# Padding keys of the later head pairs by one bf16 product over three exact parts

## The chip, the core and the metric

The kernel runs on one core of a Trainium2 chip. The metric is the device time of one execution in microseconds, taken as the median of several runs. Five engines work side by side, each through its own instruction list in order: TensorE (PE in the profile, with its weight loads as PEld), VectorE (DVE), ScalarE (ACT), GpSimd (POOL) and SyncE (SP, which here only issues DMAs). They meet through semaphores.

## The reference, cut to what matters

Two parts follow each other. The first is attention in chunks of 32 tokens, for 4 x 8 = 32 heads of 768 tokens and 64 channels. Each chunk sees eight learned memory keys of its head and the keys from 16 tokens before it to 8 tokens behind it:

```python
for c in range(nc):
    l_start = max(0, c_start - left_ctx)
    r_end = min(S, c_end + right_ctx)
    k_full = np.concatenate([mem_k, k[:, :, l_start:r_end]], axis=2)
    v_full = np.concatenate([mem_v, v[:, :, l_start:r_end]], axis=2)
    scores = scale * np.matmul(q_c, k_full.transpose(0, 1, 3, 2))
    a = softmax(scores)
    out[:, :, c_start:c_end] = np.matmul(a, v_full)
```

The second is a mixture of eight experts with one expert for each of the 3072 tokens: a gate (a product with `w_gate` plus a bias by modality) chooses the expert, and the token goes through that expert's two layers, 512 to 1024 to 512 channels, scaled by the gate. All is in fp32.

## The kernel before, in words

**Stages.** Attention goes over 16 pairs of heads (`u`, 0 to 15), each in two halves (`hf`) of twelve chunks, so that the loop counter `i` runs over 32 units and two more. Pair n's keys are turned at `i` = 2n - 2. While the pairs run, the gate of each batch of four pairs is computed in between (`route`). At the end of the attention stage the experts begin: a static list of slots of 256 tokens, with weights loaded by number of the expert, and rows gathered and scattered by GpSimd.

**Order.** Every engine's order is written out by hand: the order of the calls in the Python source is the order on each engine. A DMA on SP waits until the DMA eight places before it is done, since eight semaphores go round.

**The loop of a pair.** In the first half of pair u (even `i`) TensorE does: `scores` (L328), the transposes of the softmax input (`trans_p`, L345), the keys of the next pair (`trans_k`, L310 and L314), the transposes of the normalized output (`trans_x`, L382), the product with the values (`attend`, L357). In the second half (odd `i`) the place of the keys is taken by the queries of the next pair (`trans_q`, L292). PSUM has four banks `tr` that go round, so `trans_k` of head 1, `trans_k` of head 0 and the two halves of `trans_q` take the same banks in turn: the second half of `trans_q` can't start before ScalarE has copied head 0's keys out.

**The step that is changed.** `trans_k` puts 384 turned keys of a head into a bank by three transposes (L310), and into the gaps at both ends of the row ("pads", 16 columns, four different ones repeated) a product of `mkp`, all memory keys as 128 rows of 128, with four columns of the identity (`ident`) as the selector (L314). The result is four memory keys' channels, exact in fp32, there where the first and the last chunk would else read outside the sequence. `store_k` (L320) then copies windows of the bank into the block-diagonal key tile `kbd`, for pairs 5 and later all four copies on ScalarE. For a fp32 product the trace has two weight loads and two matmuls.

**GpSimd in the attention stage** does, for each pair: `share_v` (L271, two copies, one for a head, each behind the DMA that brings the values), the store of the output (`store_x`, L375), `mem_keys` (L302, two copies of memory keys into `kbd`). At `i` = 8 it also does `bias_rows` (L239 to L243).

**SP in the attention stage** issues, for each pair: six loads of values (L255 to L257), two copies of the memory values (L264), one load of keys and one of queries (L94). At `i` = 1 four small loads stand among them (L171 to L174).

Of the kernel before, what the change touches and what calls it, by code (L numbers as in the profile page):

```python
# [9 lines left out]
F32 = mybir.dt.float32  # L10
F32R = mybir.dt.float32r
U16 = mybir.dt.uint16
BF16 = mybir.dt.bfloat16
# [8 lines left out]
P = 128  # L22
# [23 lines left out]
def tile_chunk_attention_top1_moe(  # L46
# [14 lines left out]
    nc = tc.nc  # L61
# [13 lines left out]
    ld = c_ld.enter_context(tc.tile_pool(name="ld", bufs=3))  # L75
# [8 lines left out]
    def bank():  # L84
        return ps.tile([P, 512], F32, name="tr", tag="tr", bufs=4)
# [3 lines left out]
    def load_qk(u):  # L89
        r0 = u * 2 * S  # L90
        q2s[u] = ld.tile([P, 6, 2 * D], F32, name="q2")
        k2s[u] = ld.tile([P, 6, 2 * D], F32, name="k2")
        for t, f in ((k2s[u], kf), (q2s[u], qf)):
            nc.sync.dma_start(t.rearrange("p (h i) e -> p h (i e)", h=2), f[r0:r0 + 2 * S].rearrange("(h p j) d -> p h (j d)", h=2, p=P))  # L94
# [12 lines left out]
    mkp = pers.tile([P, P], F32, name="mkp")  # L107
# [11 lines left out]
    for h in range(2):  # L119
        r = slice(64 * h, 64 * h + 64)  # L120
        nc.scalar.copy(kbds[1][r, :, 1 - h], zero[r].unsqueeze(2).to_broadcast([64, NCH, 64]))

    ident = const.tile([P, P], F32, name="ident")
# [50 lines left out]
        nc.sync.dma_start(rows_b[N // P:], bass.AP(tensor=m_bias.tensor, offset=0, ap=[[0, 1], [0, N // P], [1, E]]))  # L174

    memT = pers.tile([P, 16, NMEM], F32, name="memT")
    iota5 = const.tile([P, 5, 27], F32, name="iota5")
    iota3 = const.tile([P, 3, 65], F32, name="iota3")
    rev = const.tile([P, 1, E], F32, name="rev")
# [68 lines left out]
    def load_v(u):  # L248
        vw = vws[u % NVW]
        for h in range(2):  # L250
            hh = 2 * u + h
            r0 = 64 * h

            src = bass.AP(tensor=vf.tensor, offset=(hh * S + 8) * D, ap=[[D, 32], [32 * D, NCH - 1], [1, D]])
            nc.sync.dma_start(vw[r0 + 24:r0 + 56, h, 0:NCH - 1, 0:D], src)  # L255
            nc.sync.dma_start(vw[r0 + 24:r0 + 48, h, NCH - 1, 0:D], vf[hh * S + S - 24:hh * S + S])
            nc.sync.dma_start(vw[r0 + 16:r0 + 24, h, 0, 0:D], vf[hh * S:hh * S + 8])  # L257

    def load_mv(u):
        vw = vws[u % NVW]  # L260
        for h in range(2):
            hh = 2 * u + h
            r0 = 64 * h
            nc.sync.dma_start(vw[r0 + 56:r0 + 64, h].rearrange("p c d -> p (c d)"), mvx[hh // 16][8 * (hh % 16):8 * (hh % 16) + 8].rearrange("p c d -> p (c d)"))  # L264
# [39 lines left out]
    def trans_k(u):  # L304
        k2 = k2s.pop(u)
        for h in (1, 0):
            hh = 2 * u + h
            t = kts[u, h] = bank()
            for i in range(3):
                nc.tensor.transpose(t[:, 9 + i:9 + i + 3 * P:3], k2[:, 3 * h + i, :], ident)  # L310

            pads = bass.AP(tensor=t.tensor, offset=t.offset + 1, ap=[list(t.ap[0]), [392, 2], [1, 8]])
            mem_sel = ident[:, 4 * hh:4 * hh + 4].unsqueeze(1).unsqueeze(1)
            nc.tensor.matmul(pads, mkp, mem_sel.to_broadcast([P, 2, 2, 4]), start=True, stop=True)  # L314

    def store_k(u, h, j, copy):
        tt = kts[u, h][64 * j:64 * j + 64]
# [55 lines left out]
    def store_x(u):  # L373
        b, g = divmod(u, 4)
        nc.gpsimd.dma_start(xd[b * S:(b + 1) * S, g * P:(g + 1) * P].rearrange("(t p) c -> p t c", p=P), xbs[u])  # L375
# [378 lines left out]
    def conv(i, eng=None):  # L754
        nc.scalar.copy(wh[i], raw[i])  # L755
        (eng or nc.vector).tensor_sub(wl[i], raw[i], wh[i].bitcast(F32))  # L756
# [6 lines left out]
    def fetch(rows, part):  # L763
        for t in range(2):
            nc.gpsimd.indirect_dma_start(  # L765
                out=xg[t][:, part], out_offset=None, in_=rows, in_offset=bass.IndirectOffsetOnAxis(ap=gx[:, t:t + 1], axis=0))

    def gather(row, gates=True, between=()):
        if row < 2:
            src, reg, rows = table, regsb[0:1, 2:3] if row else regs0[0:1, 1:2], N - S  # L770
        else:
            src, reg, rows = tab_i, (regs1 if row < NSURE else regs)[row:row + 1, 2:3], N
        col = nc.values_load(reg, engines=[mybir.EngineType.Pool], min_val=0, max_val=E * HI,
                             skip_runtime_bounds_check_because="clamped to the table on chip")
        nc.gpsimd.tensor_copy(ix, src[:, ds(col, 2)])
        nc.gpsimd.tensor_scalar(gx, ix, float(rows - 1), None, op0=ALU.min)
        fetch(xd[0:rows], slice(0, DM))
        for step in between:
            step()
        if flipped(row):  # L780
            for t in range(2):
                flip(planes[t], xg[t], xpl[:, :, t * P:(t + 1) * P])
        if gates:
            fetch(gd[0:rows], slice(DM, XW))
# [146 lines left out]
    load_qk(1)  # L931
    load_v(1)
    trans_k(0)
    t = ps.tile([P, 512], F32, name="av", tag="av", bufs=2)
    for h in range(2):
# [34 lines left out]
    for i in range(n + 2):  # L970
        live = i < n
        u, hf = units[i] if live else (NU, i % 2)
# [101 lines left out]
        if live and hf == 0 and u >= 1:  # L1074
            if u - 1 + NVW < NU:
                load_v(u - 1 + NVW)
                load_mv(u - 1 + NVW)
            if u + 4 < NU:
                load_qk(u + 4)
        if (u, hf) == (NU - 2, 1):  # L1080
            c_ld.close()
            xp = ctx.enter_context(tc.tile_pool(name="xp", bufs=1, side="right"))
            ix = xp.tile([P, 2], I32, name="ix")
            gx = xp.tile([P, 2], I32, name="gx")
            xg = [xp.tile([P, XW], F32, name=f"xg{t}") for t in range(2)]
            xt = xp.tile([P, 4, 2, 256], F32R, name="xt")
            xth, xtl = xt[:, :, 0], xt[:, :, 1]
            w1h, w1l = [xp.tile([P, 8, 512], F32R, name=f"w1{i}") for i in range(2)]
            hh, hl = [xp.tile([P, 8, 256], F32R, name=f"h{i}") for i in range(2)]
            for f in range(8):  # L1090
                raw[f] = xp.tile([P, 512], F32, name=f"raw{f}")
                wh[f], wl[f] = w1h[:, f], w1l[:, f]
            flat = vws[1].rearrange("p h c d -> p (h c d)"), kbds[0].rearrange("p c h m -> p (c h m)")
            old = [t[:, k * 512:(k + 1) * 512] for t in flat for k in range(6)]
            raw[8:16] = old[0:8]
            load_w(0, 0, 0)
            with nc.allow_non_contiguous_dma(reason="one gate per token"):
                nc.sync.dma_start(*chosen.pop())
            gather(0, gates=False)
            for f in range(4, 8):  # L1100
                nc.gpsimd.memset(raw[f][0:1, 0:1], 0.0)
            load_w(0, 0, 1)
        elif (u, hf) == (NU - 1, 1):
            conv(0)
            other = second()
            fetch(gd[0:N - S], slice(DM, XW))
            for f in range(8, 16):
                nc.gpsimd.memset(raw[f][0:1, 0:1], 0.0)
            load_w(0, 1)
            store_x(NU - 3)  # L1110
            store_x(NU - 2)
# [220 lines left out]
```

## Time and profile before

| what | value |
|---|---|
| time, median of 3 runs | 430.8 us (430.32 to 432.37) |
| the profiled execution, its own time | 429.93 us |
| its span in the trace | 428.1 us |
| TensorE busy | 412.1 us (96%) |
| VectorE, ScalarE, GpSimd busy | 335.0, 300.2, 234.2 us |
| granted TensorE clock | 0.996 of full speed on the mean |

The span is the stretch from the first to the last instruction; 1.8 us of the execution lie around it. The attention stage is about the first 123 us, the experts are the rest. A busy share tells little about what a change is worth: what counts is which engine the others wait for at each place, which the chain of waits and the timelines of the engines tell.

### The profile page before, as it was taken

What the parts mean: (1) busy time and instruction counts of PE and PEld (TensorE: products, weight loads), DVE (VectorE), ACT (ScalarE), POOL (GpSimd) and SP (SyncE); (2) the same over time, 40 slices, a digit from 0 to 9 for tenths busy, and PEclk for the clock granted to TensorE, in tenths of its full rate; (3) what the DMA queues carried; (4) which work ended last, traced back from release to release, by engine and by line L of the source; (5) the groups of instructions that cost most, each with busy time, mean ns of one, the idle gap of its engine ahead of it and who ended that gap; (6) DMA issues with size and microseconds to landing.
All of it is one profiled execution on the core that took longest, in us unless ns stands there. A gap on an engine that the chain in (4) does not pass through costs nothing.

```text
span 428.1 us, 11395 instructions
## 1 busy us (share of the span) xinstructions
PE 412.1 (96%) x3867; PEld 342.2 (80%) x3870; DVE 335.0 (78%) x800; ACT 300.2 (70%) x597; POOL 234.2 (55%) x320
## 2 busy tenths in 40 slices
PE   7998999999999999999999999999999999999993
PEld 4776788877867888899898888888888778888882
DVE  6899588588787789858979887868985887978750
ACT  7787778687655557557566867868784778878750
POOL 8967678669584409666753466452706566520101
PEclk9999999999999999999999999999999999999998
DMA  9889999999659500335423667979938323320101
GB/s 218 184 217 246 229 273 201 258 255 212 133 132 312 176 2 2 100 99 76 92 82 52 270 192 167 332 207 334 277 143 253 98 72 84 86 64 2 50 3 55
DMA packets 82543, 66.81 MB, mean 156 GB/s; under 512 B 50659, under 2 KB 71339, under 8 KB 82476
## 3 DMA queue, kind: packets, MB, share of 16 engines
q1 hardware_dynamic: 75276, 46.36, 44.4%
q0 software_dynamic: 6784, 19.50, 14.5%
q8 instruction: 33, 0.54, 0.6%
q14 instruction: 34, 0.28, 0.2%
q10 hardware_dynamic: 416, 0.13, 0.1%
HBM read 84.64 MB, written 12.76 MB: 228 GB/s over the span
## 4 chain that ended last, share of the span: by engine, by line
PE 57%; issue 16%; DVE 10%; DMA 6%; ACT 5%; POOL 4%; POOLq 0%; SPq 0%; ACTq 0%; DVEq 0%
PE av L856 11%; PE tr L844 9%; PE sc L856 8%; PE tr L825 7%; PE av L357 4%; PE tr L828 4%; PE sc L328 3%; ACT kbd L320 3%; PE tr L382 2%; PE tr L345 2%; DMA xpm<-xw 2%; PE tr L292 2%; PE tr L310 1%; DMA out_dram<-o,ix_now 1%; POOL xg L765 1%
## 5 line engine op out<-in xcount | busy, mean ns | idle before, releaser
L756 DVE TENSOR_TENSOR w<-raw,w 128x512 fp32r<-128x512 f32 x96 | 67.4, 746 | 4.1 <-ACT w L755 3.6
L825 PE MATMUL tr<-xt,w 128*128 128x512 f32 x256 | 70.3, 396 | 0.0
L856 PE MATMUL av<-wh,h 128*128 128x512 f32 x192 | 62.5, 398 | 0.0
L271 POOL COPY vw<-vw 24x1472 f32<-24x1472 f32 x32 | 45.0, 1408 | 18.9 <-DMA vw<-in_v_dram 17.5
L755 ACT CAST w<-raw 128x512 fp32r<-128x512 f32 x96 | 53.9, 619 | 0.6 <-DMA raw<-in_moe_w_dram 0.6
L856 PE MATMUL sc<-wh,h 128*128 128x512 f32 x160 | 51.7, 398 | 0.0
L825 PEld LDWEIGHTS tr<-xt,w 128*128 128x128 f32 x256 | 44.3, 189 | 7.5 <-DVE hs L834 0.7
L844 PE MATMUL tr<-xt,w 128*128 128x256 f32 x384 | 48.2, 285 | 1.2 <-DVE xt L820 0.7
L844 PEld LDWEIGHTS tr<-xt,w 128*128 128x128 f32 x384 | 46.8, 191 | 2.7 <-DVE xt L820 0.9
L320 ACT COPY kbd<-tr 64x672 f32<-64x672 f32 x57 | 44.6, 782 | 2.9 <-PE tr L314 1.3
L828 PEld LDWEIGHTS tr<-xt,w 128*128 128x128 f32 x256 | 39.3, 189 | 5.4
L856 PEld LDWEIGHTS av<-wh,h 128*128 128x128 f32 x192 | 36.1, 188 | 8.4 <-issue 0.2
L861 POOL DMA_INDIRECT out_dram<-o,ix_now x22 | 24.5, 1112 | 29.8 <-ACT o L860 24.1
L828 PE MATMUL tr<-xt,w 128*128 128x256 f32 x256 | 40.7, 281 | 0.0
L856 PE MATMUL av<-wl,h 128*128 128x512 f32 x96 | 38.1, 397 | 0.2 <-DVE wl L756 0.2
L834 DVE TENSOR_TENSOR hs<-tr,hs 128x256 f32<-128x256 f32 x64 | 26.8, 419 | 14.4 <-ACT hs L831 14.3
L856 PEld LDWEIGHTS sc<-wh,h 128*128 128x128 f32 x160 | 30.1, 188 | 7.1 <-issue 0.2
L835 ACT ACTIVATE h<-hs 128x256 fp32r<-128x256 f32 x64 | 26.8, 419 | 12.7 <-DVE hs L834 11.6
L837 DVE TENSOR_TENSOR wl<-vw,wh 128x512 fp32r<-128x512 f32 x48 | 34.0, 709 | 2.1
L838 DVE SCALAR_TENSOR_TENSOR h<-hs,h 128x256 fp32r<-128x256 f32 x64 | 27.3, 426 | 7.7 <-ACT h L835 7.7
L765 POOL DMA_INDIRECT xg<-xd,gx x24 | 27.6, 1149 | 10.3 <-issue 5.5
L347 ACT ACTIVATE PT<-tr 128x384 f32<-128x384 f32 x32 | 15.8, 495 | 23.2 <-PE tr L345 23.0
(265 smaller groups left out, 911.1 us busy)
## 6 DMA issues: line engine op xcount, KB each, us to landing
raw<-in_moe_w_dram SPq DMA_DIRECT2D x96, 256.0 KB
vw<-in_moe_w_dram SPq DMA_DIRECT2D x72, 256.0 KB
k<-in_k_dram SPq DMA_DIRECT2D x16, 384.0 KB
q<-in_q_dram SPq DMA_DIRECT2D x16, 384.0 KB
xd<-xb POOLq DMA_DIRECT2D x16, 384.0 KB, 5.9
kbd<-in_moe_w_dram SPq DMA_DIRECT2D x24, 256.0 KB
vw<-in_v_dram SPq DMA_DIRECT2D x32, 184.0 KB
xall<-in_moe_w_dram SPq DMA_DIRECT2D x4, 1024.0 KB
```

Source lines behind the costliest of these rows:

```text
L271: nc.gpsimd.tensor_copy(vw[r0:r0 + 24, h, 1:NCH, 0:D], vw[r0 + 32:r0 + 56, h, 0:NCH - 1, 0:D])
L320: copy(dst.rearrange("p c (i j) -> p c i j", j=2)[:, :, :, j], win)
L755: nc.scalar.copy(wh[i], raw[i])
L756: (eng or nc.vector).tensor_sub(wl[i], raw[i], wh[i].bitcast(F32))
L765: nc.gpsimd.indirect_dma_start(out=xg[t][:, part], out_offset=None, in_=rows, in_offset=bass.IndirectOffsetOnAxis(ap=gx[:, t:t + 1], axis=0))
L825: nc.tensor.matmul(ph, wh[f][:, c * P:(c + 1) * P], xt[:, c].rearrange("p a n -> p (a n)"), start=(c == 0), stop=False, skip_group_check=True)
L828: nc.tensor.matmul(ph[:, 0:256], wl[f][:, c * P:(c + 1) * P], xth[:, c], start=False, stop=(c == 3), skip_group_check=True)
L834: nc.vector.tensor_add(hs, ph[:, 0:256], hs)
L837: nc.vector.tensor_sub(wl[w], raw[w], wh[w].bitcast(F32))
L838: nc.vector.scalar_tensor_tensor(hl[:, f], hs, 0.0, hh[:, f].bitcast(F32), op0=ALU.max, op1=ALU.subtract)
L844: nc.tensor.matmul(ph, w[f][:, c * P:(c + 1) * P], x[:, c, :], start=(n == 0), stop=(n == 11))
L856: nc.tensor.matmul(pos[t], x, w[8 + f], start=(f == 0 and n == 0), stop=(f == 7 and n == 2))
```

## The change

From pair 6 on, the sixteen pad columns come from a bf16 product. Each fp32 memory key is split into three bf16 parts whose sum is the key (first the key rounded to bf16, then the rest rounded, then what is left). The parts stand in `bits`: partitions 0 to 31, 32 to 63 and 64 to 95 hold part one, two and three of eight heads' keys (32 rows of 128), with four such groups side by side for 32 heads, and zeros in the last 32 partitions. `pick3` is a 32 x 32 identity three times over, so that one product adds the three parts of the four rows that it picks. Pairs 0 to 5 keep the fp32 product.

The parts are made at the beginning: three DMAs of 64 KB on SP at `i` = 1, behind the load of keys and queries of pair 4, bring the same 32 rows to three places of `mem3`; GpSimd splits them in three steps at the ends of `i` = 4, 6 and 8.

```diff
     memT = pers.tile([P, 16, NMEM], F32, name="memT")
+    mem3 = ld.tile([96, 4, P], F32, name="mem3", bufs=1)
+    bits = ld.tile([P, 4, P], BF16, name="bits", bufs=1)
+    pick3 = ld.tile([P, 32], BF16, name="pick3", bufs=1)
+
+    def load_mem3(k):
+        src = bass.AP(tensor=mem_k.tensor, offset=0, ap=[[P, 32], [32 * P, 4], [1, P]])
+        nc.sync.dma_start(mem3[32 * k:32 * k + 32], src)
+
+    def split_mem3(step):
+        pool, two, three = nc.gpsimd, slice(32, 64), slice(64, 96)
+        if step == 0:
+            pool.memset(bits, 0.0)
+            pool.memset(pick3, 0.0)
+            for k in range(3):
+                pool.tensor_copy(pick3[32 * k:32 * k + 32], ident[32 * k:32 * k + 32, 32 * k:32 * k + 32])
+            pool.tensor_copy(bits[0:96], mem3)
+        elif step == 1:
+            pool.tensor_sub(mem3, mem3, bits[0:96])
+            for r in (two, three):
+                pool.tensor_copy(bits[r], mem3[r])
+        else:
+            pool.tensor_sub(mem3[three], mem3[three], bits[three])
+            pool.tensor_copy(bits[three], mem3[three])
...
             pads = bass.AP(tensor=t.tensor, offset=t.offset + 1, ap=[list(t.ap[0]), [392, 2], [1, 8]])
-            mem_sel = ident[:, 4 * hh:4 * hh + 4].unsqueeze(1).unsqueeze(1)
-            nc.tensor.matmul(pads, mkp, mem_sel.to_broadcast([P, 2, 2, 4]), start=True, stop=True)
+            if u < 6:
+                mem_sel = ident[:, 4 * hh:4 * hh + 4].unsqueeze(1).unsqueeze(1)
+                nc.tensor.matmul(pads, mkp, mem_sel.to_broadcast([P, 2, 2, 4]), start=True, stop=True)
+            else:
+                mem_sel = pick3[:, 4 * (hh % 8):4 * (hh % 8) + 4].unsqueeze(1).unsqueeze(1)
+                nc.tensor.matmul(pads, bits[:, hh // 8], mem_sel.to_broadcast([P, 2, 2, 4]), start=True, stop=True)
...
+        if i == 1:
+            for k in range(3):
+                load_mem3(k)
+        if i in (4, 6, 8):
+            split_mem3(i // 2 - 2)
```

Three places show how the order moves. First TensorE, before the change, at the keys of pair 6 (`i` = 10); `k_603` is the key tile of that pair, and the brackets name the engines or DMA queues that the instruction waits for:

```order
L345 MATMUL tr<-ident,sb 128x128 x2
L310 MATMUL tr<-ident,k_603 128x128 [waits DMAHW2_49,PE_49]
L310 MATMUL tr<-ident,k_603 128x128 x2
L314 MATMUL tr<-ident,mkp 128x2x8
L310 MATMUL tr<-ident,k_603 128x128 [waits PE_49]
L310 MATMUL tr<-ident,k_603 128x128 x2
L314 MATMUL tr<-ident,mkp 128x2x8
L382 MATMUL tr<-ident,xb 128x128 [waits DVE_49,Activation_49]
```

The same place after it, with the lines' new numbers (L310 is L333 now, L314 is L341, L345 is L372, L382 is L409):

```order
L372 MATMUL tr<-ident,sb 128x128 x2
L333 MATMUL tr<-ident,k_609 128x128 [waits DMAHW5_49,PE_49]
L333 MATMUL tr<-ident,k_609 128x128 x2
L341 LDWEIGHTS bits [waits Pool_49]
L341 MATMUL tr<-pick_148,bits 128x2x8
L333 MATMUL tr<-ident,k_609 128x128 [waits PE_49]
L333 MATMUL tr<-ident,k_609 128x128 x2
L341 LDWEIGHTS bits
L341 MATMUL tr<-pick_148,bits 128x2x8
L409 MATMUL tr<-ident,xb 128x128 [waits DVE_49,Activation_49]
```

The fp32 product became one weight load and one matmul, and the first weight load waits for GpSimd; no other wait of TensorE is added in the whole program.

GpSimd before, from the memory keys of pair 3 (L302, `kbd_111`) to the values of pair 5 (L271, `vw_114`):

```order
L302 COPY kbd_111<-memT 64x24x8 x2
L271 COPY vw_112<-vw_112 24x23x64 x2
L375 DMA xd<-xb 128x6x128
L302 COPY kbd_110<-memT 64x24x8 x2
L271 COPY vw_113<-vw_113 24x23x64 x2
L375 DMA xd<-xb 128x6x128
L302 COPY kbd_111<-memT 64x24x8 x2
L239 MEMSET mods 25x128
L240 CAST mods<-mod_i 24x128
L241 TENSOR_TENSOR bias_b<-bias_b 24x8
L243 TENSOR_TENSOR rows_b<-bias_b,ident 24x192
L271 COPY vw_114<-vw_114 24x23x64 x2
```

GpSimd after, first from the memory keys of pair 3 (now L325) to the second step of the split:

```order
L325 COPY kbd_111<-memT 64x24x8 x2
L188 MEMSET bits 128x512
L189 MEMSET pick_148 128x32
L191 CAST pick_148<-ident 32x32 x3
L192 CAST bits<-mem_146 96x512
L294 COPY vw_112<-vw_112 24x23x64 x2
L402 DMA xd<-xb 128x6x128
L325 COPY kbd_110<-memT 64x24x8 x2
L194 TENSOR_TENSOR mem_146<-mem_146,bits 96x512
```

The first step of the split stands ahead of the values of pair 3 (now L294), and its last copy, from the loaded keys, holds the engine until the three DMAs are there. Then, still after the change, the second and the third step:

```order
L194 TENSOR_TENSOR mem_146<-mem_146,bits 96x512
L196 CAST bits<-mem_146 32x512 x2
L294 COPY vw_113<-vw_113 24x23x64 x2
L402 DMA xd<-xb 128x6x128
L325 COPY kbd_111<-memT 64x24x8 x2
L262 MEMSET mods 25x128
L263 CAST mods<-mod_i 24x128
L264 TENSOR_TENSOR bias_b<-bias_b 24x8
L266 TENSOR_TENSOR rows_b<-bias_b,ident 24x192
L198 TENSOR_TENSOR mem_146<-mem_146,bits 32x512
L199 CAST bits<-mem_146 32x512
L294 COPY vw_114<-vw_114 24x23x64 x2
```

The second step stands ahead of the values of pair 4, the third behind `bias_rows` and ahead of the values of pair 5; the copy at L199 is the one that TensorE waits for. On SP the three DMAs stand between the queries of pair 4 and the values of pair 3, and nothing else moves; VectorE and ScalarE keep their lists.

## Rows read from the trace of the kernel before

**Rows 1.** Page: shares of the chain that ended last, by engine.
```profile
PE 57%; issue 16%; DVE 10%; DMA 6%; ACT 5%; POOL 4%; POOLq 0%; SPq 0%; ACTq 0%; DVEq 0%
```

**Rows 2.** Chain that ended last (start us, length us, work): unit 7, pair 10, rank products.
```profile
36.46 0.80 PE av L357 x24
...
75.71 0.33 PE tr L310 x3
76.04 0.13 PE tr L314 x2
76.17 0.37 PE tr L310 x3
76.54 0.13 PE tr L314 x2
...
80.27 0.74 PE tr L292 x6
...
89.73 0.13 PE tr L577 x6
```

**Rows 3.** TensorE's timeline at the next pair's queries (start, length, instructions, idle before).
```profile
49.78 0.92 PE L292 MATMUL tr<-ident,qr 128*128 128x128 f32 x6
...
65.40 0.55 PE L292 MATMUL tr<-ident,qr 128*128 128x128 f32 x3 [0.25 <-ACT kbd L320]
...
72.40 1.05 PE L292 MATMUL tr<-ident,qr 128*128 128x128 f32 x6
```

**Rows 4.** ScalarE's timeline in pairs 6 and 8.
```profile
46.00 3.22 ACT L320 COPY kbd<-tr 64x672 f32<-64x672 f32 x4
...
61.65 0.49 ACT L347 ACTIVATE PT<-tr 128x384 f32<-128x384 f32 x1 [1.32 <-PE tr L345]
62.16 3.19 ACT L320 COPY kbd<-tr 64x672 f32<-64x672 f32 x4
```

**Rows 5.** TensorE's timeline: first pad product of pair 6.
```profile
45.55 0.29 PE L314 MATMUL tr<-ident,mkp 128*128 128x16 f32 x2
```

**Rows 6.** GpSimd's timeline, 32 to 43 us.
```profile
32.06 1.41 POOL L271 COPY vw<-vw 24x1472 f32<-24x1472 f32 x1 [0.24 <-DMA vw<-in_v_dram]
...
34.34 0.74 POOL L302 COPY kbd<-memT 64x192 f32<-64x192 f32 x2
37.51 2.88 POOL L271 COPY vw<-vw 24x1472 f32<-24x1472 f32 x2 [2.43 <-DMA vw<-in_v_dram]
...
42.84 0.51 POOL L243 TENSOR_TENSOR rows_b<-bias_b,ident 24x192 f32<-24x192 f32 x1
```

**Rows 7.** GpSimd's groups by line and form (count, busy us, mean ns of one, idle before).
```profile
L271 POOL COPY vw<-vw 24x1472 f32<-24x1472 f32 x32 | 45.0, 1408 | 18.9 <-DMA vw<-in_v_dram 17.5
...
L673 POOL TENSOR_SCALAR a<-iota,ac,tokm 128x192 fp32r<-128x192 f32 x10 | 10.7, 1070 | 0.0
L302 POOL COPY kbd<-memT 64x192 f32<-64x192 f32 x28 | 10.1, 361 | 5.9 <-PE sc L328 4.5
...
L243 POOL TENSOR_TENSOR rows_b<-bias_b,ident 24x192 f32<-24x192 f32 x1 | 0.5, 505 | 0.1
...
L241 POOL TENSOR_TENSOR bias_b<-bias_b 24x8 f32<-24x8 f32 x1 | 0.2, 196 | 0.0
```

**Rows 8.** DMA view, 20 to 50 us, all packets; and SP's timeline, one issue.
```profile
DMA packets 9751, 7.07 MB, mean 236 GB/s; under 512 B 6826, under 2 KB 9392, under 8 KB 9744
...
25.08 0.42 SPq L255 DMA_DIRECT2D vw<-in_v_dram  x1
```

**Rows 9.** VectorE's timeline: a small copy beside GpSimd's copy, and a maximum.
```profile
30.71 1.13 DVE L223 CAST tab_i<-table 128x2 int32<-128x2 f32 x1
...
36.31 0.55 DVE L336 TENSOR_REDUCE mx<-sc 128x6 f32<-128x384 f32 x1
```

**Rows 10.** GpSimd's timeline ahead of that, and TensorE's at unit 7.
```profile
30.41 1.41 POOL L271 COPY vw<-vw 24x1472 f32<-24x1472 f32 x1 [3.15 <-DMA vw<-in_v_dram]
...
37.85 0.55 PE L345 MATMUL tr<-ident,sb 128*128 128x128 f32 x3
```

## The prediction

> **What bounds the kernel now.** I read the page first: the chain that ended last is TensorE's for 57% and ScalarE's for 5% [rows 1]. That says that time taken from TensorE can count, not that it does. So I went to the chain in order of time, in the attention stage, where the changed products stand, and then to the timelines of the engines beside TensorE, to see at each pair who arrives last.
>
> Around the pad products the chain is TensorE's in pair 10: three transposes, 0.13 us for the two records of a fp32 pad product, three transposes, 0.13 us again [rows 2]. But the next thing that TensorE does with the same PSUM banks is to turn the queries of that pair, and the second half of that waits until ScalarE has copied the keys out. In pair 8 TensorE stands idle there for 0.25 us, behind ScalarE's copies [rows 3]; pairs 7, 11, 12 and 14 read the same, with 0.21, 0.24, 0.22 and 0.55 us. ScalarE in turn is one unbroken run: from the exponential at 61.65 us through four copies until 65.35 [rows 4]. That run starts with trans_p, ahead of the keys, so it doesn't feel how long a pad product takes. In these pairs ScalarE sets the pace, and TensorE has time to spare. In pair 9 the six query transposes take 1.05 us in place of some 0.92 [rows 3], the same wait hidden in a longer group; pairs 13 and 15 read alike. Only in pairs 6 and 10, alike, do the six run through without a wait [rows 3]: there TensorE has the gate's products to do in between, ScalarE is done at 49.22 us [rows 4], and the second three transposes start at about 50.15 (half of the 0.92 us group behind 49.78), so ScalarE is early by about 0.9 us.
>
> **What it removes.** Twenty fp32 pad products, two in each of ten pairs. In pair 10 the stretch is 0.33 + 0.13 + 0.37 + 0.13 = 0.96 us; six transposes alone take 0.74 [rows 2]. Two pad products are worth 0.22 us, 0.11 each. What takes their place is like the rank products, bf16 with a weight load of their own, of which six take 0.13 us, 0.022 each [rows 2]. The trace has no bf16 product among fp32 transposes: I bound it by 0.022 below and by the fp32 price 0.11 above (then nothing is gained), and take 0.025 as the rank products are nearest in form. The saving is 2 x (0.11 - 0.025) = 0.17 us for a pair, bounds 0 and 0.18. Over ten pairs that is 1.7 us of TensorE's time. On the path lie pairs 6 and 10 alone: **0.34 us**. In the other eight the same 0.17 us only makes the wait for ScalarE longer.
>
> **What it adds on SP and the DMA engines.** Three issues and 3 x 64 KB = 197 KB, ahead of the values of pair 3. At the stretch's 236 GB/s [rows 8] these are 0.83 us. Bounds: 0 if they fill a gap, 1.3 us if SP's three issues, 0.42 us each [rows 8], are what counts. I take 0.83. Who waits: GpSimd, whose second copy for pair 3 was let go by its DMA at 32.06 [rows 6], so now at 32.9. TensorE needs the values at 36.46, when pair 3's product begins [rows 2], and GpSimd is done with them 1.41 us after its DMA, at 34.3: the delay is covered by some two microseconds.
>
> **What it adds on GpSimd.** A copy costs (1408 - 361) / (1472 - 192) = 0.82 ns per element over some 0.2 us, so 0.62 us for 512 elements; a two-input operation (505 - 196) / (192 - 8) = 1.68 ns per element, so 1.04 us for 512 [rows 7]. Step one (two fills, three small copies, one copy of 512) lies in the 3.15 us in which GpSimd waits for the values of pair 3 [rows 10], and costs nothing there but the arrival of its own three DMAs, which the 0.83 us hold already. Step two is 1.04 + 2 x 0.62 = 2.3 us, step three 1.04 + 0.62 = 1.66 us.
>
> **The new wait.** TensorE's weight load for pair 6 waits for step three. I follow GpSimd: values of pair 3 done at 32.9 + 1.41 = 34.3; store and memory keys, 1.6 us (from 32.06 + 1.41 = 33.47 to 34.34 + 0.74 = 35.08 before) [rows 6], until 35.9; step two until 38.3. The values of pair 4 were there at 37.51 [rows 6], now at 38.3, so this costs nothing more. From 37.51 to 43.35 (42.84 + 0.51) GpSimd ran without a stop [rows 6]; now that stretch is 38.35 to 44.2. Step three with its gaps is 1.8 us: bits are there at 46.0. TensorE wants them at 45.55 [rows 5]. It waits **0.45 us**, in pair 6, where TensorE sets the pace, and behind the weight load stand head 0's keys, trans_x, the product with the values and the gate's products. Bounds: nothing if the DMAs delay nothing (GpSimd 0.8 us earlier); on the other side a subtraction could cost as much per element as the dearest row, 1070 ns for 192 [rows 7], so 2.85 us in place of 1.04, and bits would be there at 46.0 + 2 x 1.81 = 49.6, a wait of 4.1 us. I take the two-input row, the same operation in fp32.
>
> **The sum.** 0.45 - 0.34 = +0.1 us. Against the profiled execution (429.93 us) that is 430.0; the median of the runs is 0.9 us above it, so on the median 430.8 + 0.1 = 430.9.
>
> **The shared port.** VectorE's copy of two columns took 1.13 us, from 30.71 to 31.84, and GpSimd's copy ran from 30.41 to 31.82 [rows 9, 10]. So VectorE can stand behind a GpSimd instruction, and GpSimd has more of them now. The Trainium skill, "SBUF — State Buffer", section "Who interferes with whom", says that a VectorE instruction in a two-port mode and a GpSimd instruction shut each other out for a whole instruction. It speaks against this change; by that rule the time would be the third rival's. The trace agrees for the copy of two columns.
>
> **Rivals.** *All pairs pay.* If the waits for ScalarE shrink with TensorE's work, or bits come in time and every pair gives 0.17 us, the gain is 1.7 us: 429.1, at the bound of 0.18 a little under. For it speaks that the chain names the pad products in most pairs; against it, the waits in eight of ten pairs.
> *Bits in time, VectorE freed.* Step one's own wait moves the values of pair 3 to about 31.2 us. The copy of two columns, which lost 1.0 us behind them [rows 9], is then through before. VectorE is on the chain there; with 0.34 us from TensorE and 0.7 of the 1.0 kept this is 429.8. It needs bits before 45 us, 1 us earlier than my sum.
> *VectorE blocked.* Step two's subtraction begins at 35.9, just when three small VectorE operations stand ahead of the maximum of unit 7 at 36.31 [rows 9]. If they wait until it ends, the maximum is 0.9 us late and the transposes at 37.85 [rows 10] by 0.5; four small operations near 28 us meet step one's copies, some 0.6 together. Pair 6 is then 1.1 us late by VectorE, which hides the wait for bits: 1.1 - 0.34 = +0.8, 431.6.
> *Bits very late, slower.* The single mechanism is GpSimd's price for mixed fp32 and bf16 operands. At the upper bound the wait is 4.1 us: +3.7, 434.5; half way it is 2.3 us: +1.9, 432.7. It decides for slower at all from bits at 45.9 us on, and for a loss of 0.5% from 48.0. Against it: copies and two-input operations are the cheaper rows.
> *The product isn't cheaper.* Then nothing is saved and 0.45 us is lost: 431.3.
>
> **How the numbers follow.** Forecast (429.9 to 431.6, nearly no change) 0.47; all pairs pay 0.12; bits in time with VectorE freed 0.11; VectorE blocked 0.12; bits very late 0.13; product not cheaper 0.05. The likeliest gives 430.9. The range from 429.0 to 432.8 takes in all but the far half of "all pairs pay" and of "bits very late", and the 2 us by which the runs of before differ among themselves. 0.5%, about what a measurement of this kernel can tell from no change, is 2.15 us, so under 428.6 and over 433.0. Faster by more needs all pairs and something else on top, the freed VectorE: 0.08. Slower by more is half or more of "bits very late" with a part of the blocked case: 0.12. The rest, 0.80, is within.
>
> **What would show it.** In the new trace: the pad product as one record of a bf16 product, with some 0.03 us on the chain, shows the price; the idle time of TensorE ahead of the query transposes at 0.35 to 0.45 us in pairs 7, 8, 11 and 12 shows that the saving went into the wait for ScalarE; a wait of TensorE for GpSimd of about half a microsecond at 45 to 46 us, once, shows the third step late; two subtractions at 1.0 us and copies at 0.6 show GpSimd's prices. I am wrong if those waits for ScalarE stay as they are and the stage ends earlier by over a microsecond; or if the subtractions take two microseconds and more; or if the values of pair 3 or 4 now hold TensorE, which no term of mine allows.

## The result: 0.5% slower, and where the time stands in the new profile

The changed kernel takes 433.53 us on the median of 22 runs (429.96 to 435.53), the kernel before 431.42 us on the median of 22 runs. The ratio is 1.0052, interval 1.0032 to 1.0073: some 2.2 us slower. The prediction was 430.9 in a range from 429.0 to 432.8; the measured time lies beyond its slow end. Two further measurements, on two chips, gave 1.0048 (1.0028 to 1.0067) and 1.0017 (0.9987 to 1.0046); the second can't be told from no change.

The profiled execution took 430.76 us, only 0.8 us above that of before. So there are two questions: where the 0.8 us come from, and why the medians lie 2.1 us apart.

In the new page, the shares of the chain that answer to [rows 1]:

```profile
PE 51%; issue 15%; DVE 10%; ACT 8%; DMA 6%; POOL 6%; SPq 1%; POOLq 0%; ACTq 0%; DVEq 0%
```

TensorE's share fell from 57% to 51%, ScalarE's rose from 5% to 8%, GpSimd's from 4% to 6%. The lines have moved: L310 is now L333, L314 is L338 (fp32) and L341 (bf16), L292 is L315, L320 is L347. TensorE's timeline after the change, as [rows 5] and [rows 3] (start, length, instructions, idle before); the first keys of pair 7 and of pair 15 stand at 55.81 and 117.57 us:

```profile
45.27 0.49 PE L333 MATMUL tr<-ident,k 128*128 128x128 f32 x3
47.40 0.18 PE L341 MATMUL tr<-pick,bits 128*128 128x16 bf16 x1 [1.64 <-POOL bits L199]
...
55.81 0.49 PE L333 MATMUL tr<-ident,k 128*128 128x128 f32 x3
...
59.79 0.55 PE L315 MATMUL tr<-ident,qr 128*128 128x128 f32 x3 [0.44 <-ACT kbd L347]
...
117.57 0.49 PE L333 MATMUL tr<-ident,k 128*128 128x128 f32 x3
```

The same keys of pairs 7 and 15 before the change:

```profile
54.21 0.49 PE L310 MATMUL tr<-ident,k 128*128 128x128 f32 x3
...
115.99 0.49 PE L310 MATMUL tr<-ident,k 128*128 128x128 f32 x3
```

The first bf16 product of pair 6 waits 1.64 us for the last step of the split. Then, in pairs 7 and 8, the wait for ScalarE's copies is 0.44 us (59.79 and 66.97) where it was 0.21 and 0.25 [rows 3]. From pair 7's first key transpose to pair 15's it takes 61.76 us, and 61.78 before (54.21 to 115.99): the cheaper product brought nothing there. At pair 7 the changed kernel is 1.60 us late (55.81 against 54.21), at pair 15 1.58 us. Of this 0.8 us is left at the end; what gives back the rest, behind the attention stage, was not tried.

GpSimd's timeline, as [rows 6]:

```profile
33.05 1.81 POOL L294 COPY vw<-vw 24x1472 f32<-24x1472 f32 x1 [1.13 <-DMA vw<-in_v_dram]
...
36.57 1.16 POOL L194 TENSOR_TENSOR mem<-mem,bits 96x512 f32<-96x512 f32 x1
37.80 1.25 POOL L196 CAST bits<-mem 32x512 bf16<-32x512 f32 x2
39.11 3.09 POOL L294 COPY vw<-vw 24x1472 f32<-24x1472 f32 x2
...
45.20 1.15 POOL L198 TENSOR_TENSOR mem<-mem,bits 32x512 f32<-32x512 f32 x1
46.42 0.93 POOL L199 CAST bits<-mem 32x512 bf16<-32x512 f32 x1
```

The parts are ready at 47.35 us; the prediction had 46.0.

### The profile page after: what moved, and what is told of

Read it like the earlier page. It is cut to its first block, busy times and chain, and to the rows that moved or that the text cites. A ratio compares the mean times of both kernels' runs of the same rounds, so it can differ in the third digit from the quotient of the medians.

```text
span 428.8 us, 11371 instructions
## 1 busy us (share of the span) xinstructions
PE 409.3 (95%) x3850; PEld 339.4 (79%) x3850; DVE 330.0 (77%) x800; ACT 300.1 (70%) x597; POOL 245.2 (57%) x331
## 3 DMA queue, kind: packets, MB, share of 16 engines
q0 software_dynamic: 6784, 19.50, 14.2%
## 4 chain that ended last, share of the span: by engine, by line
PE 51%; issue 15%; DVE 10%; ACT 8%; DMA 6%; POOL 6%; SPq 1%; POOLq 0%; ACTq 0%; DVEq 0%
PE av L883 11%; PE tr L871 8%; PE sc L883 8%; PE tr L852 7%; ACT kbd L347 5%; PE tr L855 4%; PE av L384 2%; PE sc L355 2%; POOL xg L792 2%; DMA xpm<-xw 2%; DMA vw<-in_moe_w_dram 2%; PE tr L372 1%; PE tr L315 1%; DMA out_dram<-o,ix_now 1%; PE tr L409 1%
## 5 line engine op out<-in xcount | busy, mean ns | idle before, releaser
L783 DVE TENSOR_TENSOR w<-raw,w 128x512 fp32r<-128x512 f32 x96 | 65.6, 728 | 4.1 <-ACT w L782 3.6
L294 POOL COPY vw<-vw 24x1472 f32<-24x1472 f32 x32 | 46.1, 1440 | 11.9 <-DMA vw<-in_v_dram 10.5
L347 ACT COPY kbd<-tr 64x672 f32<-64x672 f32 x57 | 44.6, 782 | 4.1 <-PE tr L341 1.6
L817 POOL COPY planes<-xg 128x1024 uint16<-128x1024 uint16 x18 | 22.4, 1255 | 18.5 <-DMA xg<-xd,gx 18.5
```

Of the source, the lines that this page charges most:

```text
L294: nc.gpsimd.tensor_copy(vw[r0:r0 + 24, h, 1:NCH, 0:D], vw[r0 + 32:r0 + 56, h, 0:NCH - 1, 0:D])
L347: copy(dst.rearrange("p c (i j) -> p c i j", j=2)[:, :, :, j], win)
```

## Experiments: the wait, the clock behind it, the split, and ScalarE

Three theories stood against each other. Theory A: the time is the wait in pair 6 and what follows from it. Theory B: the loads and GpSimd's work cost by themselves. Theory C: the difference of the medians is scatter of the clock.

**The changed kernel again (e1).** No edit.

> The changed kernel once more, as the measure for the others of this set. Theory A (the wait for bits): its trace shows TensorE idle for 1.5 to 1.8 us once, ahead of the first bf16 pad product, and its median is 1.0 to 2.5 us above the kernel before. Theory B (GpSimd's and the DMA engines' added work slows the stage by itself): the same sum, but only part of the 1.6 us stands at that wait. Theory C (the difference between the medians, 2.1 us, against 0.8 between the two profiled executions, is scatter of the granted TensorE clock): the ratio comes out under 1.003 this time.

Measured: 433.21 us against 431.18, ratio 1.0048. Its profiled execution, span 432.2 us, shows what the first one didn't. TensorE's timeline, and a table by stretches (length, busy time of PE, PEld, DVE, ACT, POOL with counts, then the granted clock, DMA share, GB/s):

```profile
46.25 0.49 PE L333 MATMUL tr<-ident,k 128*128 128x128 f32 x3
48.53 0.18 PE L341 MATMUL tr<-pick,bits 128*128 128x16 bf16 x1 [1.79 <-POOL bits L199]
...
49.46 1.53 PE L384 MATMUL av<-vw,PT 128*32 128x130 f32 x24
50.77 2.43 PE L561 MATMUL tr<-xall,wg 128*32 128x384 f32 x16
53.02 0.83 PE L355 MATMUL sc<-kbd,qT 128*32 128x128 f32 x24
```
```profile
49.30:52.70 3.40, 3.40 (x41) 1.81 (x42) 0.92 (x3) 3.31 (x6) 3.23 (x5) 0.50 1.30 267
52.70:60.00 7.30, 7.30 (x136) 6.31 (x132) 3.84 (x13) 3.70 (x9) 4.61 (x6) 1.00 1.07 241
```

Behind 1.79 us of idle TensorE, up to 48.53 us, the granted clock is still 1.00 until 49.30, then 0.50, which is 1.2 GHz, for 3.4 us. The product with the values there takes 1.31 us from start to start and the gate's products 2.25, in place of 0.69 and 1.29 at 1.00 in the first trace: 1.6 us lost on top of the wait. Where the clock falls, only a trace shows; of the other executions the mean clock alone is on record, and 3.4 us at half the clock take some 0.004 from it (an estimate: 1.7 of 432 us). The kernel before has 0.995 to 0.999 in all 35 runs of this set; the changed kernel has 0.994 or less in 15 of its first 22 runs and in 9 of these 12. These 24 have a median of 433.8 us, the ten others 431.8. So the clock does scatter, as C says, but in this set it is low in most runs of the changed kernel and in none of the kernel before.

This trace also shows something that speaks for theory B. Pair 6's keys begin at 46.25 us, 1.0 us later than before, still ahead of the new wait. GpSimd began the second copy of pair 3's values at 34.69 us, where the first trace had 33.05, and TensorE stood idle for its memory keys, 0.70 us ahead of 37.76 and 0.28 us ahead of 45.07. GpSimd's and TensorE's timelines:

```profile
34.69 1.42 POOL L294 COPY vw<-vw 24x1472 f32<-24x1472 f32 x1 [0.46 <-DMA vw<-in_v_dram]
...
37.76 0.86 PE L355 MATMUL sc<-kbd,qT 128*32 128x128 f32 x24 [0.70 <-POOL kbd L325]
```

**From pair 7 on (e2), the split without its use (e3), bias_rows earlier (e4).**

```diff
-            if u < 6:
+            if u < 7:       (e2)
+            if u < NU:      (e3: fp32 pads everywhere)
```
```diff
-        if i == 8:
+        if i == 4:          (e4)
             bias_rows()
```

> The bf16 product starts one pair later, so that TensorE wants the parts at about 52.9 us, 5.5 us after they are ready. Theory A: no wait for GpSimd; the stage ends 1.5 us or more earlier than in the changed kernel, and against the kernel before only the saving of pair 10 is left: -0.2 us, ratio 0.998 to 1.001. Theory B: still 1 to 2 us slower than before, ratio 1.003 to 1.005. If every pair paid, the eight ACT-bound pairs would give 0.2 us each: -1.8 us against before, ratio 0.996.

> The loads and the three steps of the split stay, but all pads come from the fp32 product, so nobody waits for the parts. Theory A: as the kernel before, ratio 0.999 to 1.001. Theory B: 1 to 2 us slower, ratio 1.003 to 1.005.

> The changed kernel with bias_rows (1.3 us of GpSimd, 43.84 to 45.15) moved from i = 8 to i = 4, ahead of step one, where GpSimd waits 0.54, 0.67 and 1.13 us for DMAs. The parts should be ready at 47.35 - 1.3 = 46.0 us. Theory A: the wait in pair 6 shrinks from 1.64 to some 0.3 us, the time by 1.3 us against the changed kernel; ratio to the kernel before 1.000 to 1.002. Theory B: bias_rows costs as much at its new place; the ratio stays at 1.003 to 1.005. A third reading, that GpSimd's instructions after 39 us only meet VectorE's copies at other times: the wait shrinks by under 0.8 us.

Measured: e2 431.51 us, ratio 1.0007 (0.9980 to 1.0034); e3 431.43, 1.0015 (0.9992 to 1.0039); e4 431.08, 1.0006 (0.9988 to 1.0025); before 431.18. Three different ways to take the wait away each take 1.7 to 2.1 us from the changed kernel's 433.21. The mean clock is 0.995 or more in 11, 9 and 12 of their 12 runs; what lowers it in three runs of e3, which never waits for the parts, no trace shows. That is theory A for the main part; the intervals leave room for some tenths of a microsecond of B. But none of the three is faster than before, though e2 and e4 have the cheap product in nine or ten pairs.

In e4 the wait for the parts is gone, and TensorE waits twice for VectorE instead. TensorE's, VectorE's and GpSimd's timelines at the second of these:

```profile
39.28 0.52 PE L372 MATMUL tr<-ident,sb 128*128 128x128 f32 x3 [0.96 <-DVE den L392]
...
36.93 1.15 DVE L259 SCALAR_TENSOR_TENSOR quarter<-pcol,quarter 128x1 f32<-128x1 f32 x2
...
36.81 1.25 POOL L196 CAST bits<-mem 32x512 bf16<-32x512 f32 x2
```

Two operations on one column, 0.52 us in the changed kernel, take 1.15 us and end with GpSimd's casts. The wait at 30.89 us in the same trace (0.73) goes back to a VectorE operation of 1.06 us beside bias_rows and the fills of step one. This is the rival "VectorE blocked", in a kernel in which bias_rows stands earlier in GpSimd's list.

**The wait filled (e5, and e13 and e14 on one chip).**

```diff
+            if u == 6 and h == 1:
+                spare.append(bank())
+                warm(spare[0], 7)
             pads = bass.AP(tensor=t.tensor, offset=t.offset + 1, ...
```

> The changed kernel, with seven idle bf16 products of 512 columns put ahead of pair 6's first pad product, between the key transposes and the wait for the parts, so that TensorE works in the time in which it would wait. The trace of the changed kernel that was run again shows, behind 1.79 us of idle TensorE, a stretch of 3.4 us in which the granted clock is 0.50 (1.2 GHz); there the product with the values and the gate's products take 1.6 us more. Theory (the idle wait is what lowers the clock, and that is why the medians differ by 2.1 us and the profiled executions by 0.8): TensorE arrives at the pad product as late as before, but the clock stays at 1.00 there in the trace, nearly all runs list 0.995 or more (in the changed kernel 24 of 34 list 0.994 or less), and the median is 0.7 to 1.2 us under the changed kernel's, ratio to before 1.002 to 1.004. Rival (the clock falls by itself, in some runs, whatever TensorE does): as many low clocks as in the changed kernel, ratio 1.005.

> The changed kernel, beside e14 and e15 on one chip. If the chip holds the clock at the level of before in the kernel before: ratio 1.004 to 1.006, over half of the runs with a mean clock of 0.994 or less, where the kernel before has nearly none. If the clock falls in the kernel before too, as on the chip of the last set, the difference shrinks to what the wait itself costs, 1.001 to 1.003.

> The changed kernel with seven idle products in the wait, on the same chip. Theory (idle TensorE lowers the clock): low clocks are as rare as in the kernel before, and the time is 0.7 to 1.6 us under the changed kernel's of this set. Rival (no link): the same clocks and the same time as the changed kernel, within 0.4 us.

Measured: e5 431.63 us against 431.08 on its chip, 1.0018 (0.9992 to 1.0043), and 0.994 or less in 1 of 12 runs. TensorE's timeline:

```profile
45.53 1.67 PE L306 MATMUL tr<-idle 128*128 128x512 bf16 x6
47.47 0.18 PE L344 MATMUL tr<-pick,bits 128*128 128x16 bf16 x1 [0.27 <-POOL bits L199]
```

TensorE reaches the pad product at 47.47 us, as late as in the changed kernel, but with little idle time, and the clock stays at 1.00 until the last microseconds. On this chip the kernel before has 0.994 or less in 2 of 32 runs; the changed kernel itself was not measured there. On the chip of e13 and e14 the changed kernel takes 440.06 us and the filled one 438.44, 1.6 us less, ratios 1.0017 (0.9987 to 1.0046) and 0.9987 (0.9962 to 1.0012); the intervals overlap. There the clock falls in the kernel before too (0.987 to 0.994 in 35 runs), so another bound was chosen, after the result: 0.985 or less in none of its 35 runs, in 5 of 12 of the changed kernel, in 1 of 12 of the filled one. Together this speaks strongly for the idle wait as what brings the clock down, but the link is not a rule for each execution: e13's trace has a wait of 1.78 us and no fall behind it.

The trace of e14 shows the same link at another place. There TensorE waits 2.04 us for the values of pair 3, and behind that the granted clock is 0.53, nearly the lower level, for 3.6 us; the wait for the parts is filled, and no fall follows it. TensorE's timeline and the table by stretches:

```profile
37.14 1.29 PE L387 MATMUL av<-vw,PT 128*32 128x130 f32 x24 [2.04 <-DMA vw<-in_v_dram]
```
```profile
37.40:41.00 3.60, 3.60 (x56) 3.22 (x46) 2.12 (x6) 0.35 (x1) 2.80 (x5) 0.53 0.97 204
```

**The split's own price (e11, e12, e15).** The kernel of e3 twice more, and e12 with the three DMAs alone:

```diff
-        if i in (4, 6, 8):
-            split_mem3(i // 2 - 2)
```

> The loads and the split alone, with fp32 pads everywhere, once more, since its interval (0.9992 to 1.0039) left open whether they cost anything. If they cost nothing: 0.999 to 1.001, and the mean of both measurements under 1.001. If VectorE and TensorE lose time to GpSimd's added instructions and to the DMAs: 1.001 to 1.003 again.

> The three DMAs of the memory keys alone, with nothing split and fp32 pads everywhere. If the 197 KB on the DMA engines are what costs: as with the split, 1.001 to 1.002. If GpSimd's instructions are: 0.999 to 1.001, under the kernel with the split. If neither costs anything, both are at 1.000.

> The loads and the split with fp32 pads, on the same chip. If they cost something by themselves: 1.0015 to 1.003, 0.6 to 1.3 us. If not: 0.999 to 1.001.

Measured: e11 441.27 us against 439.60, 1.0031 (1.0003 to 1.0060); e12 439.41, 1.0004 (0.9976 to 1.0032); e15 439.78 against 438.68, 1.0003 (0.9977 to 1.0029). The mean of e3, e11 and e15 is 1.0016, 0.7 us. In the times, the loads cost nothing that can be told, and the split may cost up to a microsecond.

The traces say more of theory B than the times. From pair 4's to pair 6's first key transpose, ahead of any use of the parts, the four traces of kernels without the loads (before, e6, e9, e16) take 14.2 to 15.2 us, the fourteen with them 14.5 to 17.3, nine of them over 15.7 and e12, with the loads alone, 17.3. In most of those nine GpSimd gets the values of pair 3 late, and TensorE waits for the DMAs of that pair or for the memory keys that GpSimd copies behind them: 1.64 and 0.72 us in e12, 1.06 and 0.73 in e11. The loads are not needed for such a wait (e16 has 0.72 us too), but with them it is commoner in these traces. How much of this is left at the end of the execution stays open.

**ScalarE relieved (e6, e7).** The second copy of head 1's keys left out in pairs 7 to 15, once in the kernel before and once with bf16 products from pair 7 on. The keys that it brings are missing there.

```diff
-            store_k(u + 1, 1, 1, nc.scalar.copy if u > 3 else nc.vector.tensor_copy)
+            if u < 6:
+                store_k(u + 1, 1, 1, nc.scalar.copy if u > 3 else nc.vector.tensor_copy)
```

> The kernel before, without the second copy of head 1's keys (0.8 us of ScalarE) in pairs 7 to 15; the keys that it would bring are left out there. From TensorE's first key transpose of pair 7 to that of pair 15 the kernel before takes 61.78 us. Theory (ScalarE sets the pace in these pairs): TensorE's waits ahead of the second half of the query transposes go (0.21 to 0.55 us in a pair), the stretch takes 60.0 to 60.8. Rival (VectorE or the transfers set it): within 0.3 of 61.8.

> The same copy left out of the kernel that uses the bf16 product from pair 7 on. The changed kernel takes 61.76 us for the stretch from pair 7's to pair 15's first key transpose, 0.02 under the kernel before, though its pad products are 0.23 us shorter in each pair. Theory (the saving went into the wait for ScalarE): with ScalarE relieved it comes out, and the stretch is 1.2 to 1.8 us shorter than in the fp32 kernel with the same copy left out. Rival (the saving is lost elsewhere, as at VectorE or in slower products): the two stretches agree within 0.4 us.

Measured: the fp32 kernel takes 428.02 us, ratio 0.9946 (0.9917 to 0.9974), and its stretch from pair 7 to pair 15 is 58.96 us, 2.8 under before, more than expected. The bf16 kernel takes 431.21 us, 1.0015 (0.9988 to 1.0042), its stretch 60.92 us: not shorter but longer. A part of this can be read. In pairs 8 and 11 the two agree to the hundredth, 6.21 and 6.43 us. ScalarE's and TensorE's timelines in pair 8, with ScalarE's copy of the turned outputs, which stands behind its three key copies, and TensorE's query transposes and trans_x, first of e6, then of e7:

```profile
63.45 0.48 ACT L385 COPY xall<-tr 128x384 f32<-128x384 f32 x1
...
63.54 0.82 PE L292 MATMUL tr<-ident,qr 128*128 128x128 f32 x6
64.19 0.49 PE L382 MATMUL tr<-ident,xb 128*128 128x128 f32 x3
```
```profile
65.89 0.48 ACT L412 COPY xall<-tr 128x384 f32<-128x384 f32 x1
...
65.76 0.82 PE L315 MATMUL tr<-ident,qr 128*128 128x128 f32 x6
66.64 0.52 PE L409 MATMUL tr<-ident,xb 128*128 128x128 f32 x3
```

In both, trans_x starts 0.74 or 0.75 us after ScalarE begins to copy the outputs turned before, whose bank it takes. In the bf16 kernel six transposes that need 0.65 us hold TensorE for 0.88: the saving of 0.22 us is waited away one step later. With one copy less ScalarE is still the last. Only in pair 10 does the saving come out, 8.45 against 8.80 us. The rest of e7's loss lies in stalls that e6 doesn't have, 0.49 and 0.22 us for VectorE in pair 7 and 1.12 us between the keys of pairs 13 and 14 that the trace puts down to "issue"; why they are there stays open.

**That copy on VectorE (e8, e9, e10, e16).** In pairs 7 to 15 with bf16 pads (e8), in pairs 10 and 14 alone in the kernel before (e9) and in e4 (e10), in pair 14 alone in the kernel before (e16).

```diff
-            store_k(u + 1, 1, 1, nc.scalar.copy if u > 3 else nc.vector.tensor_copy)
+            store_k(u + 1, 1, 1, nc.scalar.copy if u > 3 and u not in (9, 13) else nc.vector.tensor_copy)   (e9, e10)
```

> The bf16 product from pair 7 on, and the second copy of head 1's keys on VectorE in place of ScalarE in pairs 7 to 15, a version that may beat both kernels. If VectorE has room for 0.86 us more in a pair (it is busy 31 of 40 us between 60 and 100), ScalarE is done earlier, the waits go, and the time is 1.5 to 3 us under before, ratio 0.993 to 0.997. If VectorE is late by it (its normalization of the previous unit stands behind that copy), TensorE waits for VectorE in place of ScalarE: ratio 0.999 to 1.004. I take the second as the likelier.

> The kernel before, with the second copy of head 1's keys on VectorE in pairs 10 and 14 alone, where no gate work of a batch stands in VectorE's list. Theory (ScalarE sets the pace): from pair 14's first key transpose to pair 15's the time falls from 7.53 us to some 6.7 us, as it did in the two kernels in which that copy was taken from ScalarE (6.71 and 6.70), from pair 10's to pair 11's from 8.97 to some 8.8; together -1.0 us, ratio 0.997 to 0.999. Rival (VectorE gets late by it): 1.000 or above.

> The kernel with bias_rows at i = 4 (parts ready before TensorE wants them), and the same two copies on VectorE: a version that may beat both kernels. Theory (ScalarE sets the pace, so the product's price counts in few pairs): as the fp32 version with the two copies moved, give or take 0.5 us, ratio to before 0.996 to 0.999. Rival (the bf16 product's saving comes out once ScalarE is relieved): 1.5 to 2 us under the fp32 version, 0.993 to 0.995.

> The kernel before with the second copy of head 1's keys on VectorE in pair 14 alone. Theory: 7.53 us from pair 14's to pair 15's first key transpose become 6.7, as in three traces, and the time falls by 0.8 us, ratio 0.997 to 0.999, which would beat both kernels. Rival: the 0.8 us are given back behind the attention stage, ratio 0.999 to 1.001.

Measured: e8 435.15 us, 1.0090 (1.0059 to 1.0120), worse than expected, since the copy stands behind VectorE's own work and TensorE then waits for what ScalarE does after it: 0.76 us at 67.61, ended by ScalarE's copy of the queries.

e9 gave 1.0006 (0.9974 to 1.0039), e10 0.9976 (0.9946 to 1.0006), e16 1.0007 (0.9979 to 1.0035). Pair 14 does take 6.7 us in all three traces, 0.8 less than before, but the time doesn't show it. In e10's trace the copy in pair 10 even makes the gate's products wait 1.09 us for VectorE. No version is shown to beat the kernel before.

## Why the prediction was wrong, by its steps

The prediction had the price of the product, the eight pairs paced by ScalarE and the place of the new wait right. The steps that failed are the size of that wait, put at 0.45 us and measured at 1.64 to 1.79, and TensorE's clock behind it, which the sum puts at nothing and which cost 1.6 us in e1's trace. The saving of 0.34 us and the cover for the added DMAs were wrong too.

**Price of the product: right.** From start to start, in pair 10 of the changed kernel:

```profile
77.14 0.49 PE L333 MATMUL tr<-ident,k 128*128 128x128 f32 x3
77.46 0.17 PE L341 MATMUL tr<-pick,bits 128*128 128x16 bf16 x1
77.49 0.53 PE L333 MATMUL tr<-ident,k 128*128 128x128 f32 x3
77.86 0.17 PE L341 MATMUL tr<-pick,bits 128*128 128x16 bf16 x1
77.88 0.52 PE L409 MATMUL tr<-ident,xb 128*128 128x128 f32 x3
```

The same stretch before, from its first to its last instruction:

```profile
75.55 0.49 PE L310 MATMUL tr<-ident,k 128*128 128x128 f32 x3
...
76.52 0.53 PE L382 MATMUL tr<-ident,xb 128*128 128x128 f32 x3
```

0.03 and 0.02 us for a product, as estimated from the rank products. The pair saves 0.23 us (0.74 in place of 0.97), over the bound of 0.18: the fp32 product was worth 0.14 us, not 0.11.

**Eight pairs paced by ScalarE: right.** The waits of 0.44 to 0.47 us in pairs 7, 8, 11 and 12 are those that were forecast (0.35 to 0.45), and the stretch from pair 7 to pair 15 is as long as before.

**Pairs 6 and 10 pay: wrong.** Pair 10 begins 1.59 us after that of before and pair 11 1.61, so nothing was kept in pair 10. The step looked at the second half of the query transposes for the bank of head 0's keys [rows 3, 4]. But the gate's two products take two banks in between, so that it is the transposes of the softmax input that take that bank. ScalarE's copies and TensorE after the change:

```profile
77.91 3.22 ACT L347 COPY kbd<-tr 64x672 f32<-64x672 f32 x4
81.16 0.48 ACT L412 COPY xall<-tr 128x384 f32<-128x384 f32 x1
...
80.32 0.84 PE L355 MATMUL sc<-kbd,qT 128*32 128x128 f32 x24
81.19 0.55 PE L372 MATMUL tr<-ident,sb 128*128 128x128 f32 x3
81.69 0.93 PE L315 MATMUL tr<-ident,qr 128*128 128x128 f32 x6
```

And before the change:

```profile
76.32 3.21 ACT L320 COPY kbd<-tr 64x672 f32<-64x672 f32 x4
...
78.96 0.84 PE L328 MATMUL sc<-kbd,qT 128*32 128x128 f32 x24
79.73 0.55 PE L345 MATMUL tr<-ident,sb 128*128 128x128 f32 x3
80.11 0.91 PE L292 MATMUL tr<-ident,qr 128*128 128x128 f32 x6
```

The copies end at 81.13, and the transposes start at 81.19, 0.87 us after the scores in place of 0.77; the queries start 0.50 us later in place of 0.38, just behind ScalarE's next copy, which ends at 81.64. ScalarE was early by some 0.1 us there, not 0.9 (79.53 against 79.73 before).

Pair 6 is the same where nothing waits for the parts: in e4, with the cheap product, it takes 9.03 us from its first key transpose to pair 7's (46.65 to 55.68), 8.99 before (45.22 to 54.21). In the changed kernel the saving did come out in pair 6, but only inside the wait. The first pad product there starts 2.13 us after the keys in place of 0.33, 1.80 us more, and the pair is 1.55 us longer: ScalarE's copies begin 0.23 us behind that product (47.63 us), where before they began 0.45 us behind it, when the exponential was done (46.00). So of the 0.34 us the sum may count 0.2 against a wait that costs 1.8 from start to start, and nothing without the wait.

**Added DMAs: right in one trace, not in others.** In the first trace the values of pair 3 let GpSimd go at 33.05, forecast 32.9. But the prediction says that TensorE is covered by some two microseconds, and that it is wrong if these values hold TensorE: in e14, which has the same loads, TensorE waits 2.04 us for them, and in e1 0.70 us for the memory keys that GpSimd copies after them. e12's time, 1.0004 with an interval of 0.3% on either side, shows no cost of the loads.

**GpSimd's walk, and so the new wait: mis-sized, 1.64 us for 0.45.** The parts came 1.35 us later than the walk says. Of this, about 0.15 is the DMA; 0.4 the second copy of pair 3's values (1.81 us for 1.41); 0.2 step two (2.48 for 2.3); 0.2 the copies for pair 4 (3.09 for 2.88); 0.35 step three (2.15 for 1.8), where the cast took 0.93 us. In e2 and e4 that cast took 0.60 us. The two slow copies and the cast lie beside VectorE's copies of the queries (at 33.04, 39.19 and 46.33 us). VectorE's timeline in the changed kernel, then GpSimd's and VectorE's in e2:

```profile
46.33 0.55 DVE L300 COPY qr<-q 128x768 f32<-128x768 f32 x1
...
46.98 0.60 POOL L199 CAST bits<-mem 32x512 bf16<-32x512 f32 x1
...
47.14 0.87 DVE L300 COPY qr<-q 128x768 f32<-128x768 f32 x1 [0.68 <-DMA q<-in_q_dram]
```

In the changed kernel VectorE's copy begins first, at 46.33, and takes 0.55 us, and GpSimd's cast, from 46.42, takes 0.93. In e2 the cast begins first and takes 0.60, and VectorE's copy takes 0.87. I had weighed the shared port as something that makes VectorE wait [rows 9], and left it out of GpSimd's prices. The Trainium skill, "SBUF — State Buffer", section "Who interferes with whom", says that the one that issues first blocks the other, so both directions were in it; the 0.93 us against 0.60, and 0.55 against 0.87, agree in direction; the 0.33 and 0.32 us added are somewhat less than the 0.46 and 0.44 for which the two overlap. The subtractions took 1.15 and 1.16 us where the row of 192 elements gave 1.04.

**A term that wasn't there: the clock.** The sum knew a wait, but not what an idle TensorE can cost behind it: 1.6 us in e1's trace. If the 24 of 34 runs with a low mean clock all lost that, it is 1.1 us on the mean, with the 0.8 between the profiled executions 1.9 of the 2.1 between the medians. That is an estimate: one trace of the changed kernel shows the fall behind this wait and two do not, and the 1.0 us by which e1's trace is late ahead of the wait has no place in it.

**The rivals.** "Bits very late" comes nearest with its 432.7 for a wait of 2.3 us, but by another way: no operation was dear for its mixed types. "All pairs pay" is refuted by e2 and e4. "VectorE blocked" didn't happen in the changed kernel's first trace, but it did in e4's, and in e13's the two operations that took 0.52 us there took 1.46. "Product not cheaper" is refuted.

## What to carry to other kernels

A cheaper instruction on the busiest engine is worth nothing in a pair whose end another engine sets; follow which buffer each next step takes, since the wait moves from one step to the next until it finds the late engine. Preparation on a side engine must be walked with the prices that its instructions have beside the neighbours' work, and it should be ready a microsecond or two ahead, or be used one stage later, as in e2. A wait of TensorE can cost twice, by itself and by the clock behind it: take it away, or try idle products in it, which brought 1.6 us on one chip, with intervals that overlap.

## What the runs showed of the hardware

TensorE's clock fell to 1.2 GHz for 3.4 us behind an idle time of 1.79 us (e1) and for 3.6 us behind one of 2.04 us (e14), but not behind one of 1.78 us (e13): in some executions of one program and not in others. On two other chips, those of e9 to e12 and e13 to e16, the clock falls for 3.4 to 6.8 us at the beginning of the experts in all eight profiled executions, and the kernel before takes 439 us there in place of 431. In e16 TensorE, VectorE and ScalarE stand nearly still ahead of it; what they wait for the trace doesn't show. TensorE's idle time there is 4.41 us, ended by VectorE at 133.62. The table by stretches, of e16:

```profile
129.50:133.00 3.50, 0.00 (x0) 0.00 (x0) 0.35 (x2) 0.31 (x1) 3.00 (x11) 0.99 0.84 238
133.00:140.00 7.00, 6.38 (x47) 4.72 (x51) 3.37 (x8) 2.74 (x7) 0.86 (x1) 0.52 1.04 354
```

And small VectorE operations with two inputs can take many times their price beside a GpSimd copy. In e2, at pair 7, VectorE and GpSimd:

```profile
56.35 1.44 DVE L584 SCALAR_TENSOR_TENSOR eq<-l,rev 128x48 f32<-128x48 f32 x1
...
54.85 2.88 POOL L294 COPY vw<-vw 24x1472 f32<-24x1472 f32 x2 [2.21 <-DMA vw<-in_v_dram]
```

1.44 us in place of 0.21, until GpSimd's copies end at 57.73, and TensorE waited 1.29 us for it. In the changed kernel's first trace the same operation took 0.21 us: the collision is there or not as the engines shift against each other. It may be a part of the 2 us by which runs of one kernel differ; that was not measured.
